# The last load of head weights of each layer, split by rows over chosen DMA engines

## The chip, the core and the metric

The kernel runs on one core of a Trainium2 chip. The metric is the device time of one execution in microseconds (us); lower is better. A core has a matrix engine (PE, with PEld for its weight loads), a vector engine (DVE), a scalar engine (ACT), GpSimd (POOL) and SyncE (SP), which here does nothing but issue loads. Loads are carried by 16 DMA engines that all cut their share out of each load.

## What is computed

Two layers, each an attention block with a key and value cache followed by a gated feed-forward block, for one new token of each of two sequences. The second layer uses the same weights and the same caches as the first:

```python
B, Sq, D = 2, 1, 448
H, Sk, Dh = 16, 4096, 256          # heads, cache length, head width; F = 1792
def _A_ref(x, k_cache, v_cache, wq, wo):
    q = (x @ wq).reshape(B, Sq, H, Dh).transpose(0, 2, 1, 3)
    scores = jnp.einsum("bhqd,bhkd->bhqk", q, k_cache) * (Dh ** -0.5)
    p = _softmax(scores, axis=-1)
    o = jnp.einsum("bhqk,bhkd->bhqd", p, v_cache)
    return o.transpose(0, 2, 1, 3).reshape(B, Sq, H * Dh) @ wo
def _B_ref(x, W_gate, W_up, W_down):
    gate = x @ W_gate
    h = gate * (gate > 0) * (x @ W_up)
    return h @ W_down
x = x + _A_ref(_layernorm(x), ...); x = x + _B_ref(_layernorm(x), ...)   # layer 1
x = x + _A_ref(_layernorm(x), ...); x = x + _B_ref(_layernorm(x), ...)   # layer 2, the same
```

All data are float32. The caches are 2 x 16 x 4096 x 256 values each, 134 MB for the keys and as much for the values, and each layer reads nearly all of them.

## The kernel before, in words

The work on attention goes by units: a unit is one head of one sequence, (h, b), 32 of them in each layer. The first layer takes the units upwards, `first` (line 173), the second downwards, `second` (line 174), so that what the first layer loaded last need not be loaded again. For each unit the kernel multiplies the query with the keys (`score`, line 459), takes the softmax, and weighs the values, for most units on DVE (`weigh_rows`, line 550), for the last ones on PE (`weigh`, line 506). Every second unit it multiplies a new query (`query_rows`, line 406 holds its matmul) and projects the finished head with its output weights (`project`, line 601). After the 32 units come the feed-forward block (`ffn`, line 724) with its loads `w_in` and `w_out`, and then the second layer in the same way. At the very end, four small copies of two rows each store the output (lines 814 to 816); one copy of two rows loads x at the start (line 235).

All loads go into one large tile, `arena`. `Arena` (line 62) keeps track of which parts are free. The list `pending` holds all loads in the order in which they are to be issued; `pump` (line 139) issues them one after the other on SP's queue as long as the place that the next one needs is free, and every `release` (line 169) calls it again. The issue itself is line 157. So the order of the loads is fixed, and a load is issued when what stood in its place has been used.

An entry of `pending` is a group of keys and values of a unit, a part of the feed-forward weights, or a group of head weights. Head weights come in halves: `("q", h)` is head h's part of `wq`, `("o", h)` its part of `wo`; each is 896 columns wide (`HALF`, line 32) in all 128 rows. The host (`_arrays`, line 822) lays the halves out one beside the other, in the order in which they are loaded, as `w_first` and `w_second`, so that a group is one block of columns and one load. `FIRST` and `SECOND` (lines 44 to 52) list the groups with the unit that each is put in front of (`with_weights`, line 201). The last group of `FIRST` is one half, `("o", 15)`: no unit is given, so it stands behind all keys and values of the layer, ahead of the feed-forward weights, and it is used when the layer's last head is projected. The last group of `SECOND` is three halves, `("q", 0)`, `("o", 1)` and `("o", 0)`, and stands ahead of the last two units' keys and values.

```python
FIRST += [(None, 6, [("o", H - 1)])]
SECOND += [(H * B - 2, 0, turns(DOWN, H - 2, H - 2) + [("o", 0)])]
```

A few loads are cut into two by columns (`parts`, lines 151 to 155): the last values of each layer and the last of `w_out`.

Of the kernel before, what the change touches and what calls it, by code (L numbers as in the profile page):

```python
# [14 lines left out]
B, D, H, S, DH, F = 2, 448, 16, 4096, 256, 1792  # L15
P = 128
# [15 lines left out]
HALF = 2 * D  # L32
# [5 lines left out]
def turns(heads, a, b):  # L38
    pairs = zip(heads[a + 1 : b + 2], heads[a : b + 1])
    return [half for q, o in pairs for half in (("q", q), ("o", o))]  # L40
# [3 lines left out]
FIRST = [(0, 0, [("q", 0)] + turns(UP, 0, 2))]  # L44
# [3 lines left out]
SECOND = [(2, 3, turns(DOWN, 1, 1) + [("o", H - 4)])]  # L48
SECOND += [(2, 0, [("o", H - 3), ("q", H - 4), ("q", H - 2)])]
SECOND += [(7, 2, [("q", H - 5)] + turns(DOWN, 4, 4))]  # L50
SECOND += [(2 * i + 2, 0, turns(DOWN, i, i + 2)) for i in range(5, H - 2, 3)]
SECOND += [(H * B - 2, 0, turns(DOWN, H - 2, H - 2) + [("o", 0)])]
GRAIN = 64
SLOT = 2 * HALF
SLOT_AT = (BLOCKS * NC - 2) * UNIT
# [6 lines left out]
class Arena:  # L62


    def __init__(self):
        self.free = set(range((CELL_AT + CELLS * HALF) // GRAIN))

    def grains(self, at, n):
        return set(range(at // GRAIN, (at + n) // GRAIN))

# [23 lines left out]
def two_layers(  # L94
# [10 lines left out]
    nc = tc.nc  # L105
# [20 lines left out]
    def source(key, n):  # L126
        kind, name, c = key
        if kind in "kv":
            h, b = name
            c += NC if kind == "v" else 0  # L130
            return kv_cache[b, h][:, c * UNIT : (c + n) * UNIT]
        if kind == "w":
            w, halves, at = name
            return w[:, at : at + len(halves) * HALF]
        if kind == "in":
            return w_in[:, c * SLOT : (c + n) * SLOT]
        return w_out[:, OUT[c] * D : OUT[c + 1] * D]

    def pump():
        while pending:  # L140
            (kind, name, c), n, at = pending[0]
            size = {"w": HALF, "k": UNIT, "v": UNIT}.get(kind, SLOT)
            if kind in "kv":
                last = at_of.get((kind, name, c - 1))
                at = units.find(n, last[0] // UNIT if last else None)
            if units.take(at, n * size) is None:
                return
            pending.pop(0)
            src = source((kind, name, c), n)
            dst = arena[:, at : at + src.shape[1]]  # L150
            parts = [0, src.shape[1]]
            if kind == "v" and n == 1 and c == NC - 1 and name in (first[-1], second[-1]):
                parts[1:1] = [UNIT - SHORT * DH]
            if kind == "out" and c == 3:
                parts[1:1] = [src.shape[1] - D]
            for i, j in zip(parts, parts[1:]):
                nc.sync.dma_start(dst[:, i:j], src[:, i:j])  # L157
            if kind == "w":
                keys = [(*half, 0) for half in name[1]]
            else:  # L160
                keys = [(kind, name, c + k) if k < NC else ("v", name, k - NC) for k in range(n)]
            for k, key in enumerate(keys):
                at_of[key] = at + k * size, size
# [5 lines left out]
    def release(*key):  # L169
        units.free |= units.grains(*at_of.pop(key))  # L170
        pump()

    first = [(h, b) for h in range(H) for b in range(B)]
    second = first[::-1]
# [59 lines left out]
    nc.vector.memset(found_s[: B + 1, :D], 1.0)  # L234
    nc.scalar.dma_start(found_s[:B, :D], x.rearrange("b s d -> (b s) d"))
    pump()


# [62 lines left out]
    def park(engine, k):  # L301
        engine(lots[k], lot(k))
        at, n = at_of[parked]
        if k == 3:
            at_of.pop(parked)
        units.free |= units.grains(at + (3 - k) * n // 4, n // 4)
        pump()
# [511 lines left out]
_OUTS = [((B, 1, D), "float32")]  # L819


def _arrays(np, A_x, A_k_cache, A_v_cache, A_wq, A_wo, B_W_gate, B_W_up, B_W_down, **_):

    wq = A_wq.reshape(4, Q, H, DH)
    q = [wq[:, 32 * c : 32 * c + 32].reshape(P, H, DH).transpose(1, 0, 2) for c in range(FULL)]
    q.append(wq[:, Q - R :].reshape(4, R, H, 2, P).transpose(2, 0, 3, 1, 4).reshape(H, P, P))
    wo = A_wo.reshape(H, 2, P, D)
    head = {"q": np.concatenate(q, axis=2), "o": np.concatenate([wo[:, 0], wo[:, 1]], axis=2)}
    first, second = (
        np.concatenate([head[s][h] for *_, halves in groups for s, h in halves], axis=1)  # L830
        for groups in (FIRST, SECOND)
    )
    both = [w.reshape(4, Q, F) for w in (B_W_gate, B_W_up)]
    full = [w[:, 32 * c : 32 * c + 32].reshape(P, F) for w in both for c in range(FULL)]
    full.insert(FULL, np.concatenate([w[:, Q - R :] for w in both], axis=1).reshape(P, F))
    down = B_W_down.reshape(4, D, D)
    chunks = [down[j, m * P : (m + 1) * P] for j in range(4) for m in range(FULL)]
    chunks += [np.concatenate([down[j, FULL * P :], down[j + 1, FULL * P :]]) for j in (0, 2)]
    k = A_k_cache.reshape(B, H, G, 32, 2, 16, 2, P).transpose(0, 1, 7, 4, 6, 2, 5, 3)
    found = {  # L840
        "x": A_x,
        "kv_cache": np.concatenate([a.reshape(B, H, P, S * 2) for a in (k, A_v_cache)], axis=3),
        "w_first": first,
        "w_second": second,
        "w_in": np.concatenate(full, axis=1),
        "w_out": np.concatenate(chunks, axis=1),
    }
    return {n: np.ascontiguousarray(a) for n, a in found.items()}
# [24 lines left out]
```

## Time and profile before

| what | value |
|---|---|
| median of 3 runs | 1309.89 us (1309.23 to 1310.72) |
| the profiled execution's own time | 1308.89 us |
| its span, first to last instruction | 1307.0 us |
| read from memory in the span | 559.42 MB |
| mean granted clock of PE | 0.683 |

The profile is one execution, taken by the hardware profiler. Its page gives the busy time of each engine, the DMA queues with their packets, and the chain of work that ended last; further views give groups of instructions, who waited for whom, the issues of loads with the time until they landed, and the busy time of every engine in stretches of the span that one chooses. In a row of such stretches stand the busy times of PE, PEld, DVE, ACT and POOL, each with its count of instructions, and then the granted clock of PE, the mean busy share of the 16 DMA engines, and GB/s. A packet is counted to the stretch in which it starts, so a share of a short stretch can lie a little over 1. SPq is the queue that SP issues. "Landing" is when all of a load has arrived.

### The profile page before, as it was taken

How to read it: one execution, taken by the hardware profiler on the slowest of the kernel's cores; microseconds unless marked ns; L12 is line 12 of the kernel's file. 1: busy time of each engine (PE TensorE's matmuls, PEld its weight loads, DVE VectorE, ACT ScalarE, POOL GpSimd, SP SyncE). 2: the span in 40 equal slices, each digit the busy share in tenths (PEclk: the TensorE clock that was granted, in tenths of full speed). 3: DMA queues.
4: the chain of work that ended last, by engine and by line, in shares of the span. 5: the costliest groups of instructions: out<-in, count | busy, mean ns of one | idle time of the engine just before them, and what ended most of it. 6: DMA issues, size and time to landing. Idle time of an engine off the chain costs nothing. (4 is left out here: it accounts for less than half of the span.)

```text
span 1307.0 us, 9364 instructions
## 1 busy us (share of the span) xinstructions
PE 623.4 (48%) x3676; PEld 173.6 (13%) x3676; DVE 1022.4 (78%) x568; ACT 184.4 (14%) x560; POOL 62.5 (5%) x134
## 2 busy tenths in 40 slices
PE   2434443444344255333888454352644334334487
PEld 0101111101011011101232111110111011111022
DVE  1799988997989799979312588997899799889921
ACT  1211101111011010101112110110101011011111
POOL 0200000000000000000000200000000000000000
PEclk9666657666667565666799765666665667576678
DMA  9999999999999999999999999999999999999998
GB/s 411 426 441 428 437 434 427 438 427 438 432 435 426 439 430 436 431 432 425 422 399 426 440 434 433 436 431 432 437 426 435 428 437 430 433 434 434 422 427 348
DMA packets 16192, 560.03 MB, mean 428 GB/s; under 512 B 1810, under 2 KB 2068, under 8 KB 4756
## 3 DMA queue, kind: packets, MB, share of 16 engines
q1 hardware_dynamic: 16136, 559.42, 99.5%
q8 instruction: 29, 0.48, 0.1%
q14 instruction: 15, 0.12, 0.0%
q10 hardware_dynamic: 12, 0.01, 0.0%
HBM read 559.42 MB, written 0.00 MB: 428 GB/s over the span
## 5 line engine op out<-in xcount | busy, mean ns | idle before, releaser
L541 DVE TENSOR_TENSOR arena<-arena 128x4096 f32<-128x4096 f32 x162 | 428.9, 2647 | 9.3
L554 DVE TENSOR_TENSOR arena<-arena,probs 128x7168 f32<-128x7168 f32 x54 | 410.7, 7605 | 2.9 <-ACT probs L488 2.9
L463 PE MATMUL rawb<-arena,q_pad 128*2 128x512 f32 x1024 | 178.9, 854 | 252.9 <-DMA arena<-in_kv_cache_dram 252.9
L463 PE MATMUL rawa<-arena,q_pad 128*2 128x512 f32 x1024 | 170.5, 818 | 207.0 <-DMA arena<-in_kv_cache_dram 206.9
L485 ACT ACTIVATE nm<-top,nsr 128x1 f32<-128x1 f32 x64 | 18.8, 294 | 866.6 <-POOL top L480 866.6
L586 PE MATMUL pq<-ri,row 128*128 128x1 f32 x216 | 43.3, 304 | 161.1 <-DVE ri L496 161.1
L546 DVE TENSOR_REDUCE row<-arena 128x256 f32<-128x1024 f32 x54 | 101.3, 1876 | 0.0
L558 ACT ACTIVATE arena<-arena,probs 128x256 f32<-128x256 f32 x216 | 92.1, 497 | 0.1
L406 PE MATMUL pq<-arena,xT 128*2 128x256 f32 x300 | 88.5, 468 | 7.3 <-ACT oT L597 7.3
L463 PEld LDWEIGHTS rawb<-arena,q_pad 128*2 128x2 f32 x1024 | 29.7, 106 | 401.6 <-DMA arena<-in_kv_cache_dram 284.4
L473 DVE STREAM_TRANSPOSE found_s<-rawa 128x512 f32<-128x512 f32 x32 | 22.9, 716 | 76.0 <-PE rawa L463 76.0
L480 POOL PARTITION_ALL_REDUCE top<-mx x64 | 22.5, 351 | 1129.1 <-DVE mx L478 1129.1
L463 PEld LDWEIGHTS rawa<-arena,q_pad 128*2 128x2 f32 x1024 | 29.0, 103 | 314.8 <-issue 314.0
L586 PEld LDWEIGHTS pq<-ri,row 128*128 128x128 f32 x216 | 38.7, 253 | 213.9 <-DVE ri L496 209.9
L473 DVE STREAM_TRANSPOSE found_s<-rawb 128x512 f32<-128x512 f32 x32 | 22.9, 715 | 47.7 <-PE rawb L463 47.7
L492 POOL PARTITION_ALL_REDUCE total<-rs x64 | 39.3, 614 | 67.6 <-ACT probs L488 65.5
L611 PE MATMUL y<-arena,oT 128*2 128x448 f32 x120 | 35.8, 683 | 6.8 <-ACT oT L597 6.8
L406 PEld LDWEIGHTS pq<-arena,xT 128*2 128x2 f32 x300 | 29.9, 107 | 56.2 <-issue 32.7
L488 ACT ACTIVATE probs<-found_s,nm,sr 128x32 f32<-128x32 f32 x64 | 28.1, 440 | 2.1
L569 DVE SCALAR_TENSOR_TENSOR row<-pob,ri,row 128x256 f32<-128x256 f32 x4 | 1.9, 484 | 30.5 <-ACT row L566 30.5
L390 DVE RECIPROCAL rstd<-rstd 128x2 f32<-128x2 f32 x4 | 0.7, 166 | 31.5 <-ACT rstd L387 31.5
L597 ACT ACTIVATE oT<-pq 128x2 f32<-128x2 f32 x54 | 9.3, 172 | 72.7 <-PE pq L586 72.7
(123 smaller groups left out, 269.8 us busy)
## 6 DMA issues: line engine op xcount, KB each, us to landing
arena<-in_kv_cache_dram SPq DMA_DIRECT2D x8, 4096.0 KB, 36.8
arena<-in_w_first_dram SPq DMA_DIRECT2D x4, 2688.0 KB, 15.5
arena<-in_kv_cache_dram SPq DMA_DIRECT2D x8, 1024.0 KB, 22.9
arena<-in_w_second_dram SPq DMA_DIRECT2D x3, 2688.0 KB
arena<-in_w_in_dram SPq DMA_DIRECT2D x8, 896.0 KB, 15.3
arena<-in_kv_cache_dram SPq DMA_DIRECT2D x3, 2048.0 KB, 11.9
arena<-in_w_second_dram SPq DMA_DIRECT2D x4, 1344.0 KB, 35.9
arena<-in_w_in_dram SPq DMA_DIRECT2D x3, 1792.0 KB, 28.2
```

What stands on the lines that cost most here:

```text
L406: nc.tensor.matmul(to, xT[:, c, :], w[:, at : at + n], start=(c == 0), stop=(c > FULL))
L463: nc.tensor.matmul(raw[u % 2][32 * g : 32 * g + 2, :], q_of[u][:, j, 1 - half : 3 - half], kt[:, g, :], start=(c == 0), stop=(c == NC - 1),)
L473: nc.vector.transpose(found_s, raw[u % 2])
L480: nc.gpsimd.partition_all_reduce(mx_of[u], mx, P, RED.max)
L488: nc.scalar.activation(p_of[u].rearrange("p (h t) -> p h t", h=2), s_of.pop(u), AF.Exp, bias=nm, scale=sr[:, b : b + 1], accum_out=rs)
L492: nc.gpsimd.partition_all_reduce(r_of[u], rs, P, RED.add)
L541: nc.vector.tensor_add(v[:, :n], v[:, :n], v[:, n : 2 * n])
L546: nc.vector.reduce_sum(row[:, :DH], rest, axis=AX.X)
L554: nc.vector.tensor_mul(tiles[:, :n], tiles[:, :n], p_of[u][:, :n, None].to_broadcast([P, n, DH]))
L558: nc.scalar.activation(tiles[:, t], tiles[:, t], AF.Copy, scale=p_of[u][:, t : t + 1])
L586: nc.tensor.matmul(pT_of[u][:, c : c + 1], row[:, c * P : (c + 1) * P], r_of[u] if added(u) else ones, start=not direct, stop=True,)
L611: nc.tensor.matmul(y[32 * c : 32 * c + B, :D], stat, w, start=(c == 1 and u == 1), stop=(u == n_u - 3),)
```

## The change

The last group of head weights of each layer is no longer one load of 128 rows. Rows 0 to 111 are one load as before (112 rows). Rows 112 to 127 go by themselves. In the first layer they are one load of 16 rows; in the second they are two, one of 12 rows and one of 4. For these small loads the source is written as `(r e) n -> e r n`: it has an outermost dimension of e, which is 2 for the 16 rows, 6 for the 12 rows and 2 for the 4 rows. The host deals out the rows in the matching order (`dealt`), so that each row of the arena holds what it held before. The places, the order of the other loads and all the computation are unchanged.

```diff
+REST = 16
+TO_TWO, TO_SIX = ((REST, 2),), ((12, 6), (4, 2))
...
+            split = ()
+            if kind == "w" and name[1] == [("o", H - 1)]:
+                split = TO_TWO
+            if kind == "w" and name[1][-1] == ("o", 0):
+                split = TO_SIX
             for i, j in zip(parts, parts[1:]):
-                nc.sync.dma_start(dst[:, i:j], src[:, i:j])
+                at_row = P - REST if split else P
+                nc.sync.dma_start(dst[:at_row, i:j], src[:at_row, i:j])
+                for n_rows, e in split:
+                    rows = slice(at_row, at_row + n_rows)
+                    nc.sync.dma_start(
+                        dst[rows, i:j], src[rows, i:j].rearrange("(r e) n -> e r n", e=e)
+                    )
+                    at_row += n_rows
...
+def dealt(np, rows, split):
+
+    out, at = np.array(rows), P - REST
+    for n, e in split:
+        shape = (e, n // e, rows.shape[1])
+        out[at : at + n] = rows[at : at + n].reshape(shape).transpose(1, 0, 2).reshape(n, -1)
+        at += n
+    return out
...
+    for w, groups, split in ((first, FIRST, TO_TWO), (second, SECOND, TO_SIX)):
+        n = len(groups[-1][2]) * HALF
+        w[:, -n:] = dealt(np, w[:, -n:], split)
```

## The prediction

> **What bounds the kernel now.** I read the page first, then the stretches, then the end of the chain of waits, then the last microseconds in stretches of one microsecond.
>
> ```profile
> span 1307.0 us, 9364 instructions
> PE 623.4 (48%) x3676; PEld 173.6 (13%) x3676; DVE 1022.4 (78%) x568; ACT 184.4 (14%) x560; POOL 62.5 (5%) x134
> DMA packets 16192, 560.03 MB, mean 428 GB/s; under 512 B 1810, under 2 KB 2068, under 8 KB 4756
> q1 hardware_dynamic: 16136, 559.42, 99.5%
> q8 instruction: 29, 0.48, 0.1%
> q10 hardware_dynamic: 12, 0.01, 0.0%
> ```
>
> The queue of loads (q1) fills 99.5% of the time of 16 DMA engines; no compute engine is over 78%. The kernel streams 559 MB, and only the stream's bytes, pace and balance can move its end.
>
> ```profile
> 0.00:600.00 600.00, 247.33 (x1260) 66.76 (x1260) 509.97 (x247) 85.80 (x259) 28.68 (x62) 0.66 1.00 432
> 640.00:700.00 60.00, 54.96 (x554) 19.71 (x550) 15.18 (x53) 10.67 (x27) 2.20 (x6) 1.00 1.00 405
> 700.00:1240.00 540.00, 243.39 (x1316) 64.75 (x1312) 456.83 (x216) 76.37 (x239) 27.90 (x56) 0.66 1.00 433
> ```
>
> The last two columns are DMA share and GB/s: 432 and 433 in the long stretches, 405 where the first layer hands over to the second. The end:
>
> ```profile
> 1280.75 22.27 DMA arena<-in_w_out_dram
> 1303.02 0.04 issue
> 1303.06 0.97 PE pq L330 x24
> 1304.03 0.02 issue
> 1304.05 0.27 DVE found_s L812
> ```
> ```profile
> 1299.00:1300.00 1.00, 0.80 (x36) 0.80 (x40) 0.15 (x1) 0.00 (x0) 0.00 (x0) 1.00 1.00 405
> 1300.00:1301.00 1.00, 0.73 (x32) 0.46 (x20) 0.00 (x0) 0.00 (x0) 0.00 (x0) 1.00 0.74 301
> 1301.00:1302.00 1.00, 0.06 (x4) 0.06 (x8) 0.00 (x0) 0.00 (x0) 0.00 (x0) 1.00 0.59 237
> 1302.00:1303.00 1.00, 0.89 (x32) 0.62 (x32) 0.00 (x0) 0.00 (x0) 0.00 (x0) 1.00 0.38 131
> 1303.00:1304.00 1.00, 0.92 (x24) 0.40 (x24) 0.00 (x0) 0.00 (x0) 0.00 (x0) 1.00 0.01 2
> ```
>
> The last matmuls follow the landing of the last load, at about 1303.0. The DMA share falls from 1.00 to 0.74, 0.59, 0.38 and 0.01: the engines do not finish together. They stand idle, on average, 0.26 + 0.41 + 0.62 = 1.3 us before the last one ends; the earliest can be 3 us ahead, not more, since the share is still 1.00 up to 1300. A load has landed when its last engine has, so the slowest engine sets the end. Perfect balance here would be worth 1.3 us, 0.10% of the span. One thing that can set an engine back is in the q8 row: 29 fetches of instructions, one packet each, of 0.48 MB / 29 = 17 KB.
>
> **How a load is dealt.**
>
> ```profile
> L157 SPq DMA_DIRECT2D arena<-in_kv_cache_dram x78: 327/328/534, 1.2 to 1245.0; - x78
> L157 SPq DMA_DIRECT2D arena<-in_w_in_dram x11: 327/328/382, 646.1 to 1270.8; - x11
> L157 SPq DMA_DIRECT2D arena<-in_w_out_dram x10: 327/328/423, 671.4 to 1285.0; - x10
> L157 SPq DMA_DIRECT2D arena<-in_w_second_dram x7: 327/328/423, 683.1 to 1208.3; - x7
> L157 SPq DMA_DIRECT2D arena<-in_w_first_dram x6: 328/328/403, 0.7 to 645.6; - x6
> ```
>
> That is 78 + 11 + 10 + 7 + 6 = 112 loads. With 128 rows and one end mark for each of 16 engines, 112 x 144 = 16128 packets; q1 has 16136. The eight left over are two stores of two rows, and q10's 12 are three more copies of two rows (x in, two stores): four packets each, so two rows and two end marks. So a load of 128 rows gives each engine eight rows, and a copy of two rows goes to two engines. [...]
>
> **The change part by part.** A byte costs an engine 0.995 x 16 x 1307.0 / 559.42 = 37.2 us per MB, so a row of 3584 bytes costs 0.133 us and one of 10752 bytes 0.40 us.
>
> First layer, one half (448 KB, rows of 3584 bytes): all 16 engines take 7 rows instead of 8, -0.13 us; two take 8 more, 15 in all, +0.93 us. Second layer, three halves (1344 KB, rows of 10752 bytes): ten engines take 7 rows, -0.40 us; four take 9, +0.40 us; two take 7 + 2 + 2 = 11, +1.20 us. The bytes stay, so nothing is gained but balance.
>
> What this is worth hangs on whether the two, and the other four, are ahead. No view tells engines apart. Bounds: if they lead by 1.6 us or more, the slowest engine is one of the rest and the end moves by -0.13 - 0.40 = -0.53 us; if they have no lead at all in either layer, +0.93 + 1.20 = +2.13 us. For the second layer I take the mean lead, 1.3 us: the two end 1.20 - 1.3 = -0.1 us against the old end, later than the -0.40 of the rest, so this part is -0.1 us. For the first layer the nearest rows are these:
>
> ```profile
> 665.00:666.00 1.00, 0.90 (x13) 0.22 (x10) 0.00 (x0) 0.00 (x0) 0.00 (x0) 1.00 0.82 344
> 666.00:667.00 1.00, 0.99 (x6) 0.06 (x1) 0.00 (x0) 0.00 (x0) 0.00 (x0) 1.00 1.13 332
> 667.00:668.00 1.00, 0.63 (x8) 0.19 (x9) 0.00 (x0) 0.00 (x0) 0.00 (x0) 1.00 0.88 351
> ```
>
> Here, some 20 us behind the split load's issue, the rate drops from 405 to 344, 332 and 351: the early engines have run out of issued loads. That is 0.15 + 0.18 + 0.13 = 0.46 us on average over the engines, so a mean lead of about 0.5 us, and the two would come out 0.93 - 0.5 = +0.4 us behind. But the engines that are ahead stand there anyway, so the order they arrive in is partly lost, and -0.13 is as open; I take +0.1 us, between the two ends.
>
> Three more issues on SP:
>
> ```profile
> 645.64 0.33 SPq L157 DMA_DIRECT2D arena<-in_w_first_dram  x1
> 646.07 0.38 SPq L157 DMA_DIRECT2D arena<-in_w_in_dram  x1
> 649.70 0.33 SPq L157 DMA_DIRECT2D arena<-in_w_in_dram  x1
> 652.18 0.33 SPq L157 DMA_DIRECT2D arena<-in_w_in_dram  x1
> ```
> ```profile
> SPq L157 <- DMA arena<-in_kv_cache_dram: 5.4, 2, 3.2
> ```
> ```profile
> arena<-in_w_in_dram SPq DMA_DIRECT2D x4, 896.0 KB, 15.3
> ```
> ```profile
> arena<-in_w_second_dram SPq DMA_DIRECT2D x1, 1344.0 KB, 33.3
> ```
>
> At about 0.45 us each (0.33 for the issue and the gap to the next), they delay what is queued behind them on SP: the w_in loads in the first layer, key loads in the second. There is also a wait: SP's w_in issues at 649.70 and 652.18 waited for landings of earlier loads (the second fence, 640 to 700 us). The 2.48 us between them is the time of one 1024 KB load (1.05 MB / 432), so one more open load would push such issues one step, 2.5 us, later. The cover: these w_in loads land 15.3 us after issue, though 0.92 MB at 432 GB/s takes 2.1, so some 13 us of queue lie ahead of them. In the second layer the split load lands 33.3 us after its issue. I cost both at nothing; without the cover it would be up to 2.5 + 0.45 us once.
>
> Readers must now wait for two or three landings:
>
> ```profile
> 662.22 0.39 PEld L330 LDWEIGHTS pq<-arena,oT 128*2 128x2 f32 x16 [0.23 <-DVE oT L599]
> ```
> ```profile
> 1248.83 3.58 PE L406 MATMUL pq<-arena,xT 128*2 128x256 f32 x10 [0.26 <-ACT oT L597]
> ```
>
> The first reader of the half comes 16.6 us after the issue and is released by DVE, not by a load; the w_in load queued behind the half lands in about 15.3 us, so the half itself has landed by 661.4. The first reader of the second load runs at 1248.83, and the load landed at 1208.3 + 33.3 = 1241.6. A row or two more on an engine, +0.93 or +1.20, does not reach them. Nothing.
>
> Sum: -0.1 + 0.1 = 0.0 us on the profiled execution's 1308.89 us, which is 1.0 below the median of 1309.89. Forecast: 1309.9 us, no change that a measurement of this kernel could tell; I take 0.2% (2.6 us) for that bound.
>
> **The rivals.** *The two loaded engines become the slowest* (0.20): nothing excludes that they had no lead; then up to +2.13, 1311 to 1312 us, still within the bound. For it: fetches like q8's may fall to them. Against: a mean lead of 1.3 us.
>
> *The split is not dealt as written* (0.03): one engine takes all 16 rows. Then it has 7 + 16 = 23 rows instead of 8 in each layer, 15 x 0.133 + 15 x 0.40 = +8.0 us, less a lead of at most 3: 1315 us or more, slower. It decides from about (2.6 + 1.3) / 0.40 = 10 extra rows of the second layer on. Against: two-row copies are on two engines here.
>
> *Every load pays a fixed price on the stream* (0.03, slower). From rows: the stretch 640:700, with its many small loads, loses 60 x (1 - 405/432) = 3.8 us; all of it charged to the loads, some 20 issues, is 0.2 us each, +0.6 us for three; only if the price were exposed and several times that would it reach 1312.5 or more. [...] The queue's depth of 13 us and more says that it is hidden.
>
> *More than balance is gained* (0.04, faster): for 2.6 us it would have to work in the handover stage too, where 3.8 us are lost; but the slowest engine sheds only 0.13 us ahead of it. 1307 us.
>
> **How the numbers follow.** Forecast 0.70, the four rivals 0.20, 0.03, 0.03 and 0.04. Within 0.2%: 0.70 + 0.20 = 0.90; slower 0.06; faster 0.04. The range goes from -0.53 and the runs' own spread (1309.23 is 0.66 under the median), 1308.7, up to +2.13, 1312.0.
>
> **What would show it.** In the changed profile q1 should have 10 packets more: three loads more with end marks 16 + 2 and 16 + 6 + 2 for twice 16, so 42 - 32, 16146; a 16139 or so means single engines. The DMA share in the last three microseconds should fall later and more steeply if the two were ahead, or drag a tail of some per cent (two engines are 0.125) if they were not. The handover should stay at about 405 GB/s, the w_in loads at 12 us or more from issue to landing; if they drop under 5, the wait on SP has lost its cover and I am wrong on that term. A change over 2.6 us in either direction would make the prediction wrong.

## The result and the profile after

| | median | runs |
|---|---|---|
| before | 1310.30 us | 1309.23 to 1310.72 |
| after | 1320.03 us | 1319.57 to 1324.28 |

The ratio is 1.0082, with a 95% interval of 1.0072 to 1.0092: the change makes the kernel slower by about 10 us. The profiled execution of the changed kernel took 1322.18 us, with a span of 1320.4 us against 1307.0, so its profile shows 13 us, some 2 more than the median does.

On the page of the changed kernel, first the whole, then the DMA queue, and the share and rate of the stream in 40 slices of 33 us:

```profile
span 1320.4 us, 9370 instructions
PE 626.8 (47%) x3676; PEld 174.5 (13%) x3676; DVE 1022.3 (77%) x568; ACT 185.2 (14%) x560; POOL 62.5 (5%) x134
DMA  9999999999999999999999999999999999999997
GB/s 415 433 423 438 428 442 429 433 431 441 426 435 431 437 431 431 433 434 421 396 352 432 439 432 435 437 433 427 435 431 431 435 434 421 445 429 437 339 423 330
DMA packets 16202, 560.03 MB, mean 424 GB/s; under 512 B 1820, under 2 KB 2078, under 8 KB 4766
q1 hardware_dynamic: 16146, 559.42, 99.3%
```

The compute engines do what they did. The queue has 16146 packets, the 10 more that were counted out beforehand: the small loads did go to two, six and two engines. The bytes are the same, and the DMA engines are as busy as before by their share, 99.3% (99.5% before). Only the rate has two holes: 396 and 352 GB/s in the slices around the first split load, where the page of the kernel before has 422 and 399, and 339 in the slice of the second, where it has 422. Stretches of the changed kernel, wide ones first, then through the first hole and the second (the last two columns are DMA share and GB/s):

```profile
0.00:600.00 600.00, 251.10 (x1260) 66.89 (x1260) 510.01 (x247) 86.15 (x259) 28.72 (x62) 0.66 1.00 432
640.00:700.00 60.00, 53.49 (x506) 20.32 (x502) 13.50 (x50) 9.97 (x25) 2.21 (x6) 0.91 0.97 366
700.00:1240.00 540.00, 248.26 (x1356) 66.50 (x1344) 452.16 (x217) 77.49 (x241) 27.93 (x56) 0.66 1.00 433
```
```profile
654.00:656.00 2.00, 2.00 (x35) 0.61 (x33) 0.92 (x2) 0.48 (x1) 0.00 (x0) 1.00 1.05 370
656.00:658.00 2.00, 1.12 (x16) 0.60 (x8) 0.84 (x5) 0.00 (x0) 0.00 (x0) 1.00 1.03 247
658.00:660.00 2.00, 1.04 (x16) 0.31 (x16) 0.00 (x0) 0.00 (x0) 0.00 (x0) 1.00 1.02 211
660.00:662.00 2.00, 0.64 (x10) 0.28 (x12) 0.00 (x0) 0.00 (x0) 0.00 (x0) 1.00 1.06 286
```
```profile
1240.00:1242.00 2.00, 0.00 (x0) 0.00 (x0) 1.90 (x2) 0.00 (x0) 0.00 (x0) 0.50 0.85 200
1242.00:1244.00 2.00, 0.00 (x0) 0.00 (x0) 2.00 (x1) 0.00 (x0) 0.00 (x0) 0.50 0.90 183
1244.00:1246.00 2.00, 0.00 (x0) 0.00 (x0) 2.00 (x1) 0.00 (x0) 0.00 (x0) 0.50 1.01 216
1246.00:1248.00 2.00, 0.00 (x0) 0.00 (x0) 1.97 (x2) 0.00 (x0) 0.00 (x0) 0.50 1.11 217
1248.00:1250.00 2.00, 0.12 (x4) 0.11 (x8) 1.79 (x2) 0.00 (x0) 0.00 (x0) 0.50 0.82 190
```

This is the finding in one view: the DMA engines are busy (share 0.82 to 1.11) while they move about half of the usual 433 GB/s. In the holes they do not wait for issued loads; each packet takes longer. The trace keeps the size and the time of every packet: between 1238 and 1254 us those of the split load, of 10752 bytes, take 0.79 us on average, where they take 0.41 in the kernel before. In the second hole this goes on for more than 10 us, far longer than the 1.38 MB of the split load can need (6.4 us at 216 GB/s), so its neighbours in the queue are slowed too: the 32 KB packets of the key loads take 2.05 us in the same stretch, where 1.22 is usual.

Behind the first hole comes a second loss of another kind. The stretch 668 to 678, before and after:

```profile
668.00:678.00 10.00, 8.59 (x59) 2.31 (x54) 1.18 (x5) 2.15 (x4) 0.00 (x0) 1.00 1.03 407
```
```profile
668.00:678.00 10.00, 9.27 (x57) 2.41 (x56) 0.66 (x4) 2.25 (x5) 0.00 (x0) 0.76 0.82 288
```

Here the share falls too, to 0.82: the engines are short of issued loads for 1.8 us on average. PE had waited 0.96 and 2.24 us for values that landed late in the hole, and SP issued its last four `w_in` loads between 658.1 and 674.2 us instead of 656.9 to 668.4.

The last microseconds of the stream after:

```profile
1312.00:1313.00 1.00, 0.71 (x12) 0.60 (x16) 0.19 (x1) 0.00 (x0) 0.00 (x0) 1.00 0.62 244
1313.00:1314.00 1.00, 1.00 (x44) 1.00 (x48) 0.00 (x0) 0.00 (x0) 0.00 (x0) 1.00 0.54 213
1314.00:1315.00 1.00, 0.47 (x20) 0.20 (x10) 0.00 (x0) 0.00 (x0) 0.00 (x0) 1.00 0.14 56
1315.00:1316.00 1.00, 0.48 (x22) 0.49 (x25) 0.00 (x0) 0.00 (x0) 0.00 (x0) 1.00 0.13 50
1316.00:1317.00 1.00, 0.83 (x36) 0.49 (x25) 0.00 (x0) 0.00 (x0) 0.00 (x0) 1.00 0.10 31
```

A share of 0.14 to 0.10 for three microseconds is what about two of 16 engines make that are still at work while the others have ended. The balance, for whose sake the rows were moved, is worse than before.

### The profile page after: what moved, and what is told of

Read it like the earlier page. It is cut to its first block, busy times and chain, and to the rows that moved or that the text cites. A ratio compares the mean times of both kernels' runs of the same rounds, so it can differ in the third digit from the quotient of the medians.

```text
span 1320.4 us, 9370 instructions
## 1 busy us (share of the span) xinstructions
PE 626.8 (47%) x3676; PEld 174.5 (13%) x3676; DVE 1022.3 (77%) x568; ACT 185.2 (14%) x560; POOL 62.5 (5%) x134
## 3 DMA queue, kind: packets, MB, share of 16 engines
q1 hardware_dynamic: 16146, 559.42, 99.3%
HBM read 559.42 MB, written 0.00 MB: 424 GB/s over the span
## 5 line engine op out<-in xcount | busy, mean ns | idle before, releaser
L477 PE MATMUL rawb<-arena,q_pad 128*2 128x512 f32 x1024 | 173.9, 836 | 254.3 <-DMA arena<-in_kv_cache_dram 254.3
L477 PE MATMUL rawa<-arena,q_pad 128*2 128x512 f32 x1024 | 175.9, 841 | 208.8 <-DMA arena<-in_kv_cache_dram 208.8
L539 PE MATMUL poa<-arena,probs 128*2 128x512 f32 x128 | 18.2, 693 | 7.5 <-DMA arena<-in_kv_cache_dram 4.5
```

The source lines that it names most:

```text
L477: nc.tensor.matmul(raw[u % 2][32 * g : 32 * g + 2, :], q_of[u][:, j, 1 - half : 3 - half], kt[:, g, :], start=(c == 0), stop=(c == NC - 1),)
L539: nc.tensor.matmul(po_of[u][32 * t : 32 * t + 2, :], p_of[u][:, n : n + 2], vt[:, 2 * t * DH : (2 * t + 2) * DH], start=(c == 0), stop=(c ...
```

## The experiments

What the expectations call a partition is a row of the arena, which has 128. The theories, by the names that the expectations use; each is a supposition of mine. **A:** in an ordinary load of 128 rows each engine writes a group of partitions of its own, and a load with another count of rows puts rows on engines so that two of them write into one group and share its path. **A2:** it is the seven rows to an engine that are slow. **A3:** any load that is not dealt as 128 rows to 16 engines is slow. **B:** the two and six engines with extra rows become the slowest. **C:** a load more pushes SP's issues behind a wait. Differences below are medians against the kernel before in the same set of runs (1310.0 us for the first four, 1309.7 for the next four, 1310.1 for the three after them, 1310.8 for the last).

**Without two and six engines** (plain16):

```diff
-TO_TWO, TO_SIX = ((REST, 2),), ((12, 6), (4, 2))
+TO_TWO, TO_SIX = ((REST, 1),), ((REST, 1),)
...
-                    nc.sync.dma_start(
-                        dst[rows, i:j], src[rows, i:j].rearrange("(r e) n -> e r n", e=e)
-                    )
+                    nc.sync.dma_start(dst[rows, i:j], src[rows, i:j])
```

> Both layers: 112 rows and then the 16 rows as a plain load, one row on each of the 16 engines; nothing goes to two or six engines. Theory A (a load of 112 rows puts rows on engines so that two engines write into the same group of partitions and share its path at half the rate): still slow, 6 to 12 us above the kernel before, with the stretch 1240 to 1254 at about 200 GB/s. Theory B (the two and six engines with extra rows become the slowest): within 1 us of before. Theory C (one load more pushes SP's issues behind a wait in the handover): 3 to 6 us above before, all of it between 640 and 700.

1321.38 us, +11.4, ratio 1.0081 (1.0064 to 1.0099): as slow as the change, although by the edit every engine has 7 + 1 rows. In its trace the stretch 1240 to 1254 runs at 214 GB/s, as theory A expected (1230 to 1260 at 313, where the kernel before has 423). B is out as the main cause.

**One layer at a time** (first_only, second_only):

```diff
-            if kind == "w" and name[1][-1] == ("o", 0):
-                split = TO_SIX
```

and the host's dealing of `second` left out with it; second_only drops the other two lines and the dealing of `first`.

> Only the first layer's load is split (112, and 16 to two engines). Theory A: the 0.46 MB of this load at half rate is 1.1 us, but the loads beside it slow down too; 2 to 6 us above before. Theory B: 0 to 1 us. Theory C: all of the loss is here, 9 to 11 us.

> Only the second layer's load is split (112, 12 to six engines, 4 to two). Theory A: 5 to 8 us above before, since the profile after loses (424 - 373) / 424 of 56 us there, 6.7 us. Theory B: up to 1.2 us. Theory C: nothing, because SP issues the loads there 30 us ahead.

1314.16 us, +4.2 (ratio 1.0028, 1.0019 to 1.0038), and 1316.75 us, +6.8 (1.0045, 1.0030 to 1.0060). They add up to 11. Each layer pays for itself: in first_only the stretch 640 to 700 runs at 367 GB/s and 1230 to 1260 at 424, in second_only at 395 and 338. The second pays more, where SP issues 30 us ahead; C is not what costs there.

**The extra load alone** (by_columns): the kernel before, with

```diff
+            if kind == "w" and (name[1] == [("o", H - 1)] or name[1][-1] == ("o", 0)):
+                parts[1:1] = [src.shape[1] // 2]
```

> The kernel before with both loads cut into two halves by columns, all 128 rows in each: one more load in each layer, no change to which engine takes which row. Theory A and B: within 1 us of before. Theory C: slower by 3 us or more in the handover stage.

1309.72 us, -0.3, ratio 0.9995 (0.9985 to 1.0004). A load more in each layer costs nothing measurable, and nothing in the handover either: its stretch 668 to 678 has a share of 1.02 and 400 GB/s. C is out; the shortage of issued loads behind the first hole goes with the slow load, not with one issue more.

**Two halves of the rows** (halves): the kernel before, with

```diff
+            split = kind == "w" and (name[1] == [("o", H - 1)] or name[1][-1] == ("o", 0))
...
-                nc.sync.dma_start(dst[:, i:j], src[:, i:j])
+                for a, b in ((0, P // 2), (P // 2, P)) if split else ((0, P),):
+                    nc.sync.dma_start(dst[a:b, i:j], src[a:b, i:j])
```

> Both loads as 64 + 64 rows, plain; 16 engines take 4 rows of each, so every engine still moves eight rows. Theory A: the 16 engines write into half of the partitions at a time, two to each group, so the whole load runs at half rate: slower by 4 to 12 us. Theory A2 (seven rows to an engine, 112 not being a power of two, is what is slow): within 1 us of before. Theory B: within 1 us.

1321.87 us, +12.2, ratio 1.0090 (1.0075 to 1.0105). By the edit four rows to an engine and powers of two throughout, and as slow as 112 and 16 (a little above the 4 to 12 us of theory A): A2 is out.

**All 128 rows in one load, dealt otherwise** (deal16): the change with

```diff
-REST = 16
-TO_TWO, TO_SIX = ((REST, 2),), ((12, 6), (4, 2))
+REST = P
+TO_TWO, TO_SIX = ((P, 16),), ((P, 16),)
```

and no load of the rows ahead of `at_row`, since there are none.

> Both loads as one load of 128 rows, but with the source written with an outermost dimension of 16, so that 16 engines take eight rows each of a run of neighbouring partitions: same count of loads, same bytes on each engine, and only which engine writes which partition may differ from before. Theory A: slower by 3 to 12 us. Theory A2 and B and C: within 1 us of before.

1320.99 us, +11.3, ratio 1.0087 (1.0072 to 1.0102). On its page the queue has the packets and bytes of the kernel before; around the second load the stretch 1230 to 1260 is the hole again. First deal16, then before, then by_columns:

```profile
q1 hardware_dynamic: 16136, 559.42, 99.3%
```
```profile
1230.00:1260.00 30.00, 12.51 (x68) 3.82 (x68) 21.43 (x14) 4.15 (x14) 1.47 (x4) 0.66 0.99 331
```
```profile
1230.00:1260.00 30.00, 17.88 (x96) 4.61 (x96) 16.73 (x11) 2.11 (x8) 0.73 (x2) 0.60 0.99 423
```
```profile
1230.00:1260.00 30.00, 17.17 (x104) 4.53 (x108) 16.91 (x12) 2.20 (x8) 0.73 (x2) 0.67 0.98 419
```

The same number of loads and packets, the same bytes, eight rows to each of 16 engines: all that is left to differ is which engine carries which row, and with it the order in which the rows are read (low_rows, below, reads in the same manner and is not slow). That alone costs all that the change costs.

**The balance without the 112 rows** (dealt_columns):

```diff
-                at_row = P - REST if split else P
-                nc.sync.dma_start(dst[:at_row, i:j], src[:at_row, i:j])
+                m = j - (j - i) // 8 if split else j
+                nc.sync.dma_start(dst[:, i:m], src[:, i:m])
+                at_row = 0
...
-                        dst[rows, i:j], src[rows, i:j].rearrange("(r e) n -> e r n", e=e)
+                        dst[rows, m:j], src[rows, m:j].rearrange("(r e) n -> e r n", e=e)
```

with `REST = P`, `TO_TWO, TO_SIX = ((P, 2),), ((96, 6), (32, 2))`, and the host dealing the last eighth of the columns only.

> The balance of the change without its 112 rows: seven eighths of the columns as an ordinary load of 128 rows, the last eighth of the columns, all 128 rows, to two engines in the first layer, and as 96 rows to six and 32 rows to two in the second. The bytes of each engine are those of the change. Theory A: far less than the change loses, 0 to 3 us above before, since only two or six engines cross others' partitions. Theory B: as slow as the change, 9 to 11 us.

1311.94 us, +2.3, ratio 1.0017 (1.0008 to 1.0027). Four fifths of the loss are gone, and still nothing is gained. Slower packets of other loads are part of the rest: packets of loads beside the split ones, unchanged in size, take longer than usual by 0.4 us in the first layer (`w_in`, 650 to 664) and 0.7 us in the second (32 KB, 1220 to 1260), summed and divided by 16 engines, beyond what they do in the kernel before. How the remaining 1.2 us divide into the two engines' extra bytes (2.13 us was the prediction's bound for them), the slower split packets and the shorter rows, these runs do not tell.

**A load with rows of 64 KB** (big_rows): the kernel before, with one key load of the first layer as rows 0 to 111 and 112 to 127.

```diff
+            split = kind == "k" and name == (6, 0) and n == BOTH and not halved
+            if split:
+                halved.append(name)
...
-                nc.sync.dma_start(dst[:, i:j], src[:, i:j])
+                for a, b in ((0, 112), (112, P)) if split else ((0, P),):
+                    nc.sync.dma_start(dst[a:b, i:j], src[a:b, i:j])
```

> The kernel before with one key load in the middle of the first layer (8 MB, rows of 64 KB) as 112 + 16 plain rows; the head weights' loads are whole. Theory A: the price goes with the bytes: 7.3 MB at half rate is 17 us more, 12 to 25. Theory of a price per load (set-up, descriptors): at most as much as in the second layer of the change, under 7 us.

1334.36 us, +24.7, ratio 1.0183 (1.0166 to 1.0200). The price goes with the bytes: +4.2, +6.8 and +24.7 us for 112 rows of 0.40, 1.20 and 7.34 MB. That is about 3 us for each MB (2.6 to 2.8 if the 16 remaining rows are counted with it), where one at half rate would lose 2.3 (1 / 433 GB/s), and about 3 us on top for each of these three loads. It is no fixed price of a load.

The part on top is the loads beside it, by the packets of second_only's trace. The 128 rows of its split load take 0.82 us each instead of 0.41, which is 128 x 0.41 / 16 = 3.3 us for each engine. The 32 and 64 KB packets between 1220 and 1260 us take longer than their usual 1.22 and 2.42, by 3.0 us for each engine in all. Together that is 6.3 of the 6.8 us. In the first layer the shortage of issued loads behind the hole is part of it too. Why the neighbours are slowed, no run here shows.

**Whose partitions.** Three kernels cut the same key load by columns. The first half of the columns is loaded as usual; of the second half only 64 rows are, by eight engines:

```diff
...
+                for a, b in ((0, 32), (32, 64)):
+                    nc.sync.dma_start(
+                        dst[a:b, m:], src[a:b, m:].rearrange("(r e) n -> e r n", e=8)
+                    )
```

is low_rows; high_rows has `((64, 96), (96, 128))`, neighbours has `((0, 64),)`.

> One key load in the middle of the first layer: the first half of its columns as an ordinary load; the second half (rows of 32 KB) only for rows 0 to 63, as two loads of 32 rows, each dealt to eight engines, four neighbouring rows to an engine. Rows 64 to 127 of the second half are left out, and the rows are in another order than the reference needs. [...] Theory A with groups of eight neighbouring rows: two engines to a group, 8 to 12 us slower (4 MB or 262 KB an engine, 9.8 us at 26.8 GB/s, doubled). Theory A3 (any load that is not dealt as 128 rows to 16 engines is slow): 8 to 12 us slower.

> The same with rows 64 to 127 in place of 0 to 63 (rows 0 to 63 of the second half are left out): the same engines, the same bytes, other partitions. [...] If partitions played no part: as low_rows.

> As low_rows, rows 0 to 63, but as one load dealt to eight engines, eight neighbouring rows to an engine. [...] Groups of eight neighbouring rows: within 2 us. A3: slower by as much as low_rows.

| kernel | rows written | neighbouring rows to an engine | against before | ratio |
|---|---|---|---|---|
| low_rows | 0 to 63 | 4 and 4 | +0.5 us | 1.0002 (0.9993 to 1.0011) |
| high_rows | 64 to 127 | 4 and 4 | +12.3 us | 1.0096 (1.0081 to 1.0111) |
| neighbours | 0 to 63 | 8 | +12.4 us | 1.0091 (1.0074 to 1.0108) |

On their pages the queue (first low_rows and high_rows, which read the same, then neighbours), and the stretches 260 to 280 in which the cut load runs, first of low_rows and then of high_rows and neighbours:

```profile
q1 hardware_dynamic: 16216, 557.33, 99.1%
```
```profile
q1 hardware_dynamic: 16208, 557.33, 99.1%
```
```profile
260.00:270.00 10.00, 9.01 (x48) 2.57 (x48) 9.89 (x2) 2.32 (x7) 0.00 (x0) 0.66 1.04 429
270.00:280.00 10.00, 1.59 (x10) 1.02 (x8) 9.90 (x8) 1.48 (x6) 0.74 (x2) 0.77 0.98 426
```
```profile
260.00:270.00 10.00, 8.68 (x36) 3.04 (x40) 9.89 (x4) 2.32 (x7) 0.38 (x1) 0.50 1.02 213
270.00:280.00 10.00, 2.86 (x22) 1.15 (x16) 8.54 (x7) 1.00 (x4) 0.74 (x2) 0.84 1.02 220
```
```profile
260.00:270.00 10.00, 9.01 (x48) 2.45 (x47) 9.89 (x2) 2.32 (x7) 0.00 (x0) 0.66 1.02 233
270.00:280.00 10.00, 1.59 (x6) 1.02 (x8) 7.99 (x7) 1.00 (x4) 0.74 (x2) 0.76 1.10 236
```

The packets fit the edit: 64 rows and twice eight end marks are 80 more than 16136 for the first two (16216 stands on both pages), 64 and eight are 72 more for neighbours. With eight engines to a load and the same bytes, one placement runs at the full 429 GB/s and two at about half of it, 213 to 236. Loads on eight engines are not slow in themselves, so A3 is out. The groups are not eight neighbouring rows either: then neighbours would be the fast one.

The slowing is not confined to the cut load. The 64 KB packets of the load after it take 4.6 us on average between 260 and 280 in neighbours and 4.9 in high_rows, where 2.42 is usual, and the whole core is at half rate. No run here shows why.

**Written or read** (high_from_low): high_rows with

```diff
-                        dst[a:b, m:], src[a:b, m:].rearrange("(r e) n -> e r n", e=8)
+                        dst[a:b, m:], src[a - 64 : b - 64, m:].rearrange("(r e) n -> e r n", e=8)
```

> As high_rows (written are rows 64 to 127 of the arena), but read are rows 0 to 63 of the cache, the very rows that low_rows read; the rest is left out as there. If the engines meet where they write (theory A): as slow as high_rows, 10 to 14 us above before. If they meet where they read: as low_rows, within 2 us of before.

1319.87 us, +9.1, ratio 1.0068 (1.0051 to 1.0085); its two stretches:

```profile
260.00:270.00 10.00, 9.01 (x48) 2.41 (x47) 9.90 (x2) 2.32 (x7) 0.00 (x0) 0.66 1.03 226
270.00:280.00 10.00, 1.60 (x6) 1.02 (x8) 7.99 (x7) 1.00 (x4) 0.73 (x2) 0.76 0.97 242
```

It reads what low_rows read and writes where high_rows wrote, and it is slow. The slowing goes with the rows that are written (+9.1 and +12.3 us for 64 to 127), not with the rows that are read (the same as in low_rows, +0.5). The 9.1 lie a little under the 10 to 14 that were expected, and 3 us under high_rows; what makes up these 3 us stays open. Which engine carries which row, no view shows: the placements are those that the edits ask for, and the times are what speaks for them. That two engines share a path to a group of rows, as theory A supposes, no run shows; the times of low_rows, high_rows and high_from_low fit it, and that is all.

## Why the prediction was wrong

The forecast was 1309.9 us, no change; the loss is 9.7 us.

*That the stream bounds the kernel and the slowest engine its end:* right; the loss lies in the stream, in its rate in the two holes and, behind the first, in engines without an issued load. *How the change is dealt:* right as to the number of engines; 16146 packets, as counted out.

*The price of a row:* this is the step that failed. "A byte costs an engine 0.995 x 16 x 1307.0 / 559.42 = 37.2 us per MB" was read off a stream of ordinary loads of 128 rows, and was then used for rows that are dealt otherwise. In second_only a row of 10752 bytes, priced at 0.40 us, took 0.82, and the loads beside it slowed down as well. The count "a load of 128 rows gives each engine eight rows" was right and was not enough: which eight matters, as deal16 shows with eight rows to each engine and +11.3 us. The 112 rows, which I booked as -0.13 and -0.40 us of relief, are where most is lost: the split loads cost 4.2 and 6.8 us by the runs with one layer alone. The two numbers for two and six engines, over which I weighed the bounds, hardly matter: plain16 without them is as slow.

*The first layer's and second layer's balance, +0.1 and -0.1:* not to be seen. dealt_columns, which by its edit has the change's bytes per engine without the 112 rows, is 2.3 us slower, about the +2.13 that I gave for two engines without a lead, but about 1.1 us of it are slowed packets of other loads. The +2.13 adds both layers up on the same two engines, and the 11 rows in it take the two of the 4-row load to be among the six of the 12-row load; no run shows which engines they are, and the 16146 packets show only how many. The tail at the end of the changed kernel looks like that rival, but deal16, in which no engine has extra rows, ends with a tail as well:

```profile
1313.00:1314.00 1.00, 0.71 (x29) 0.62 (x31) 0.19 (x1) 0.00 (x0) 0.00 (x0) 1.00 0.14 54
1314.00:1315.00 1.00, 1.00 (x52) 1.00 (x46) 0.00 (x0) 0.00 (x0) 0.00 (x0) 1.00 0.06 23
```

So a tail also comes without extra rows on any engine, and the prediction's sign for that rival does not prove it.

*The three issues on SP at nothing:* right for the issues themselves. The wait grew as foreseen, and at first its cover held; the rows for SP's waits between 640 and 700 and for the w_in loads between 640 and 660, of the changed kernel:

```profile
SPq L165 <- DMA arena<-in_kv_cache_dram: 10.7, 4, 3.4
```
```profile
arena<-in_w_in_dram SPq DMA_DIRECT2D x4, 896.0 KB, 16.1
```

Four waits instead of two, and the loads still land 16 us after issue. by_columns, with as much of that wait (10.0 us, four times), shows no loss. What the term left out is that a slower stream uses up the cover: from 668 to 678 the engines stood without issued loads for 1.8 us on average, and the handover, which the prediction wanted at about 405 GB/s, fell to 366.

*The rival with a price per load:* it had the right sign and the wrong mechanism. Two issues more, one in each layer, cost nothing when they hold all 128 rows (by_columns, 0.9995), while halves, with two more as well, lost 12.2 us. The rival that I lacked was one in which the stream's own rate falls.

## What to carry to other kernels

Where a stream of loads is the bound, a load is not so many rows on so many engines: keep the 128 rows as the outermost dimension of both sides (deal16, with 16 there on one side, is at 1.0087), and cut loads by columns (0.9995 here) and not by rows (1.0081 to 1.0090). A DMA share near 1 does not mean a full rate (1.11 at 217 GB/s in the second hole, 1.00 at 433 elsewhere); read the GB/s beside it, and look for stretches in which the first stays and the second halves. And before moving work to balance engines by 1 us, see what the pattern that is given up was doing for the rate.

## What had not been expected of the hardware

In the placements that lost, the whole core runs at about half rate: 213 to 242 GB/s in the key loads cut for the purpose, where low_rows has 429, and about 200 in the changed kernel between 1240 and 1250 us, where 433 is usual. A split load also slows the loads beside it in the queue: in second_only its own packets lose 3.3 us for each engine and those of its neighbours 3.0. Bytes left out gain nothing here: low_rows reads 557.33 MB instead of 559.42, and the time stays (1.0002).
